# Turning the softmax's left-over columns and q as 64-row halves beside P's halves, and adding the softmax's constant on ScalarE

## The chip, the cores and the metric

The kernel runs on one core of one Trainium2 chip. The metric is the device time of one execution in microseconds, the median of three. The core has five engines that run side by side, each through its own list of instructions in order: TensorE (PE in the rows, its weight loads PEld), VectorE (DVE), ScalarE (ACT), GpSimd (POOL) and SyncE (SP, which here issues every DMA). They wait for one another through semaphores only.

## The reference, cut to what matters

Attention with a computed bias, then a feed-forward layer with a cosine gate, all in f32:

```
scores = scale * q @ k.T                       # batch 4, heads 8, sequence 576, head width 64
scores = scores + bias(head, row, column)      # a small two-layer net of log distances
scores = scores - max(scores, axis=-1)
attn   = exp(scores)
attn   = attn / (sum(attn, axis=-1) + 1e-09)
x      = (attn @ v), heads side by side        # 2304 x 512
h      = x @ w_in                              # 512 x 2048
out    = (h * cos(h)) @ w_out                  # 2304 x 512
```

## The kernel before, in words

The program has three stages: the bias tables (to about 66 us of the profiled span), attention (66 to 322 us), and the feed-forward layer (to the end). The change lies in attention alone.

Attention runs over 16 **units** `u`, each a pair of heads of one batch, and within a unit over 5 **slots** `j`. A slot takes one block of rows: `tiles = [0, 1, 4, 2, 3]`, so slots 0, 1, 3 and 4 take 128 rows of both heads, and slot 2 (tile 4) takes the last 64 rows of both heads together. `slot(i)` writes one step of a software pipeline over three jobs: `now` (job i), `last` (job i-1) and `prev` (job i-3). Each engine's list is written by hand in this order, and nothing reorders it.

TensorE's share of a slot, in order: the scores of `now` (`qk`, L394, tile `s`); the turning of `prev`'s probabilities P (`ptrans`, L456, tile `pm`); for the four tiles of 128 rows the **left-over**, columns 512 to 575 of both heads as one 128x128 block (`ptrans_left`, L469, tile `pt`); a turn of the next unit's inputs (`turn`, L188) in slots 0 to 2: k in slot 0 (four 128x128 blocks), x in slot 1 (the last 64 rows of k and q, one block), q in slot 2 (four blocks, into a spare tile of the score pool); and a part of the product with v of the unit before (`pv`, L518). P is turned by `flip` as 64-row halves: half r uses rows 64r to 64r+63 of the array and writes its own PSUM bank, `m0` or `m1`, so two halves run beside each other. Left-over, k, x and q go through the whole 128x128 array.

`ps_s`, the score pool, has two buffers: `s` of head 0 and of head 1. In slot 2 one holds that slot's scores and the other, `spare`, the turned q. So slot 3's scores of head 1 wait until ScalarE has read `spare`.

ScalarE's share of a slot: the exponentials of `last` (`softmax_exp`, L427), each followed by a read of its accumulated sum into `dn`; the copy of `m0` (`keep_main` 0, L476); then what was turned (`keep_turned`, L195, L198, L203); then a finished product (`keep_x`). VectorE's share: scores plus bias with their extreme value (L407); `dn` plus 1e-9 (L439) and its reciprocal `rc` (L442); the copy of `m1` and of the left-over (L479); steps that widen the feed-forward weights (L101 to L107). GpSimd scales P by `rc` (`norm`, L449) and splits the turned q and k in two parts (`split`, L174, L178). The split of q in slot 0 has to be done before slot 1 overwrites the tile of turned q (L198).

SyncE issues the loads in the order of the slots by `LOAD_PLAN`: q for the unit after next in slot 0, k for the third unit in slot 2 (two DMAs of the main part, two of the last 64 rows of k and q), v in slot 4 (four DMAs). In every fourth unit each slot also loads the next heads' bias (`load_bias`, three DMAs, two for tile 4). In slot 2 of odd units a weight part is loaded (`load_w`), which waits for VectorE's last widening step.

Of the kernel before, what the change touches and what calls it, by code (L numbers as in the profile page):

```python
# [9 lines left out]
F32 = mybir.dt.float32  # L10
# [3 lines left out]
AF = mybir.ActivationFunctionType  # L14
# [14 lines left out]
def kernel(  # L29
# [11 lines left out]
    nc = tc.nc  # L41
# [71 lines left out]
    with tc.manual_schedule():  # L113
# [11 lines left out]
        bp = opened(front, "bp", 11, "right")  # L125

        warm = const.tile([1, 1], F32, name="warm")
        nc.vector.memset(warm, 0.0)
# [11 lines left out]

        def load(u, x):
# [12 lines left out]
            m = 5 if x == "k" else 4  # L154
            t = (lk if x == "k" else ld).tile([128, m, 2, D], F32, tag=x, name=f"n{x}")
            for h in range(2):
                nc.sync.dma_start(out=t[:, 0:4, h], in_=pair_[h, 0:512].rearrange("(p r) d -> p r d", r=4))
            if x == "k":
# [4 lines left out]
            nat[u, x] = t  # L163

# [20 lines left out]
        def turn(u, x, ps):  # L185
# [3 lines left out]
            return ps  # L189

        def keep_turned(x, ps):
            if x == "x":
# [8 lines left out]
                return  # L201
            o = turned[x][:, 64:576] if x == "k" else turned[x][:, 0:512]
            nc.scalar.activation(  # L203
                out=o.rearrange("p (x c) -> p x c", c=4),
# [180 lines left out]
        def qk(u, j):  # L385
# [32 lines left out]
            if t == 4:  # L418
                return ps_s.tile([128, 2, 512], F32, tag="s", name="spare")[:, 0]

        P, dn, rc = {}, {}, {}

        def softmax_exp(u, j, h):
            neg, m = cur.pop((u, j, h))
            if h == 0:
# [7 lines left out]
                accum_out=dn[u, j][:, h : h + 1],  # L433
            )

        def recip(u, j, step):
            n = 2 if tiles[j] < 4 else 1
            if step == 0:
                nc.vector.tensor_scalar(dn[u, j][:, 0:n], dn[u, j][:, 0:n], 1e-9, None, ALU.add)  # L439
            else:  # L440
                rc[u, j] = sv.tile([128, 2], F32, tag="rc", name="rc")
                nc.vector.reciprocal(rc[u, j][:, 0:n], dn[u, j][:, 0:n])  # L442

# [10 lines left out]
        def flip(out, i, r):  # L454
            p = slice(64 * r, 64 * r + 64)
            nc.tensor.transpose(out, i[p], ident[p, p], tile_position=(64 * r, 0))  # L456

        def ptrans(u, j):
            ps = [ps_m.tile([128, 512], F32, tag=f"m{r}", name="pm") for r in range(2)]
            cuts = [(256 * h + 64 * c, 640 * h + 128 * c) for h in heads_of((u, j)) for c in range(4)]  # L460
            if tiles[j] == 4:
                cuts.append((256, 512))
            for o, i in cuts:
                for r in range(2):
                    flip(ps[r][:, o : o + 64], P[u, j][:, i : i + 128], r)
            return ps

        def ptrans_left(u, j, ps):
            nc.tensor.transpose(ps, P[u, j][:, 512:640], ident)  # L469

# [71 lines left out]
        PV_EARLY = [[(-1, 0, (0, 1))], [(-1, 0, (2, 3))], [(-1, 0, (4,))], [(-1, 1, (0, 1, 2))], [(-1, 1, (3, 4))]]  # L542
        LOAD_PLAN = [[(2, "q")], [], [(3, "k")], [], [(1, "v")]]
        W_PLAN = [("abs", -1), (0, 0), (0.5, 2), (1, 5), (2, 7), ("load", 7), (3, 8), (4, 11)]
        get = lambda i: jobs[i] if 0 <= i < len(jobs) else None

        def slot(i):
# [4 lines left out]
            if last:  # L552
                for h in heads_of(last):
                    softmax_exp(*last, h)
            if prev:
                if prev[1] in (0, 2):
                    alloc_half(prev[0], prev[1] // 2)
                pm = ptrans(*prev)
# [4 lines left out]
            if left:  # L563
                pl = t[:, 0:128]
                ptrans_left(*prev, pl)
            if tx:
                pt = turn(u + tu, tx, {"x": t and t[:, 128:256], "k": t, "q": spare}[tx])
            for du, hf, chunks in PV_EARLY[j]:
                if 0 <= u + du < NU:
                    pv(u + du, hf, chunks)  # L570
            if prev:
                keep_main(*prev, 0, pm[0])
            if tx:
                keep_turned(tx, pt)
# [3 lines left out]
            if last:  # L578
                recip(*last, 0)
                recip(*last, 1)  # L580
            if prev:
# [12 lines left out]
            if now:  # L594
                if i == 1:
                    load(0, "v")
                    load(2, "k")
                for du, x in LOAD_PLAN[j]:
                    if u + du < NU:
                        load(u + du, x)  # L600
                hp, b = units[u]
# [242 lines left out]
```

## Time and profile before

| | us |
|---|---|
| median of 3 runs | 727.86 |
| lowest and highest | 727.65, 728.61 |
| the profiled execution's own time | 730.44 |
| its span, first to last instruction | 728.6 |
| TensorE busy in the span | 712.5 |
| VectorE, ScalarE, GpSimd busy | 606.6, 443.9, 405.4 |

A group of the profile is named by line, engine, operation, `out<-in`, shape and count. A timeline row merges equal instructions that follow each other: its duration runs from the first start to the last end, and a bracket gives the engine's idle time before it and who ended it. Matmuls overlap, so what one costs is read from one start to the next, not from its duration.

### The profile page before, as it was taken

Reading aid. Unit: us, or ns where it says so; the run is one execution under the profiler, and the core shown is the slowest. Engines: PE = TensorE matmul, PEld = TensorE weight load, DVE = VectorE, ACT = ScalarE, POOL = GpSimd, SP = SyncE. Lnnn points to the kernel's source line nnn. Section 1 sums busy time; section 2 is a strip of 40 time slices with the busy share of each in tenths; the row PEclk is TensorE's granted clock in tenths of the full one; section 3 lists DMA queues with packets and bytes.
Section 4 is the critical chain, followed back from the end, with each engine's and each line's share of the span. In section 5 each row is a group of like instructions: output and inputs, shape, how many; then the busy total and the mean of one; then the engine's idle time right before and its main releaser. Section 6 shows DMA issues by size and latency. Waiting matters only on the chain.

```text
span 728.6 us, 15710 instructions
## 1 busy us (share of the span) xinstructions
PE 712.5 (98%) x5786; PEld 571.8 (78%) x5786; DVE 606.6 (83%) x1307; ACT 443.9 (61%) x947; POOL 405.4 (56%) x486
## 2 busy tenths in 40 slices
PE   6997999999999999999999999999999999999997
PEld 3575667766667667669989989988989989989986
DVE  8997788989889888856788789898999999966665
ACT  6897688787778878754565555445454454443342
POOL 0204678888877788874456373564554463663300
PEclk9999899999999999999999999999999999999999
DMA  6787328335432820201011010101011010011113
GB/s 202 239 303 210 91 66 229 78 82 141 135 94 64 232 47 18 76 1 30 30 50 38 32 57 29 59 30 58 30 35 53 29 59 30 0 43 45 45 43 88
DMA packets 84398, 58.65 MB, mean 80 GB/s; under 512 B 62304, under 2 KB 70624, under 8 KB 84320
## 3 DMA queue, kind: packets, MB, share of 16 engines
q1 hardware_dynamic: 84320, 57.63, 27.2%
q8 instruction: 46, 0.75, 0.4%
q14 instruction: 32, 0.26, 0.1%
HBM read 42.00 MB, written 15.61 MB: 79 GB/s over the span
## 4 chain that ended last, share of the span: by engine, by line
PE 95%; DVE 2%; POOL 1%; issue 1%; DMA 0%; ACT 0%; SPq 0%; DVEq 0%
PE ph L644 28%; PE po L699 28%; PE pv L518 13%; PE s L394 11%; PE pa L309 6%; PE pm L456 5%; PE pt L469 2%; PE pt L188 2%; DVE ht L293 1%; PE spare L188 1%; DMA lt<-in_ltab_dram 0%; POOL P L449 0%; DVE P L407 0%; DVE acc L722 0%; POOL kN L178 0%
## 5 line engine op out<-in xcount | busy, mean ns | idle before, releaser
L449 POOL TENSOR_SCALAR P<-P,rc 128x576 f32<-128x576 f32 x144 | 115.0, 812 | 75.7 <-ACT P L427 31.1
L407 DVE CUSTOM_DVE_ANT_0 P<-s,bt 128x576 f32<-128x576 f32 x144 | 103.8, 754 | 29.1 <-PE s L394 19.7
L648 ACT ACTIVATE a<-ph,quarter 128x384 int32<-128x384 f32 x96 | 55.8, 581 | 102.3 <-PE ph L644 101.0
L503 POOL TENSOR_TENSOR xs<-xT,xs 128x384 fp32r<-128x384 f32 x96 | 107.7, 1122 | 8.0
L427 ACT ACTIVATE P<-P,m 128x576 f32<-128x576 f32 x144 | 110.6, 771 | 2.1 <-DVE m L407 1.7
L644 PE MATMUL ph<-xs,wpre 128*128 128x384 f32 x576 | 109.4, 338 | 0.0
L654 DVE SCALAR_TENSOR_TENSOR r<-a,ph 128x384 f32<-128x384 int32 x96 | 52.8, 550 | 67.4 <-ACT a L648 67.2
L644 PE MATMUL ph<-xs,w 128*128 128x384 f32 x576 | 108.3, 337 | 0.0
L644 PEld LDWEIGHTS ph<-xs,wpre 128*128 128x128 f32 x576 | 101.8, 188 | 5.7 <-DVE a L663 0.9
L644 PEld LDWEIGHTS ph<-xs,w 128*128 128x128 f32 x576 | 101.5, 188 | 4.7 <-DVE a L663 0.6
L659 ACT ACTIVATE r<-r,hpi 128x384 f32<-128x384 f32 x96 | 59.3, 617 | 73.5 <-DVE r L655 73.3
L394 PEld LDWEIGHTS s<-kN,qT 64*128 64x128 f32 (+1 forms) x864 | 70.5, 188 | 40.8 <-issue 8.8
L394 PE MATMUL s<-kN,qT 64*128 64x288 f32 (+1 forms) x864 | 93.4, 315 | 4.0 <-DVE m L407 1.8
L502 POOL TENSOR_SCALAR xs<-xT 128x384 fp32r<-128x384 f32 x96 | 62.9, 656 | 39.9 <-PE ph L644 39.9
L518 PE MATMUL pv<-PT,vN 128*64 128x320 f32 (+1 forms) x512 | 76.9, 422 | 0.1
L673 DVE TENSOR_TENSOR gl<-a,gh 128x384 fp32r<-128x384 f32 x96 | 74.3, 774 | 2.2 <-ACT gh L667 2.2
L699 PE MATMUL po<-wpre,gh 128*128 128x512 f32 x288 | 75.3, 397 | 0.0
L699 PE MATMUL po<-w,gh 128*128 128x512 f32 x288 | 75.2, 395 | 0.0
L111 POOL TENSOR_TENSOR w<-wb,w 128x512 fp32r<-128x512 f32 x16 | 20.8, 1298 | 89.2 <-ACT w L109 89.2
L655 DVE SCALAR_TENSOR_TENSOR r<-a,r 128x384 f32<-128x384 int32 x96 | 60.6, 632 | 3.3
L667 ACT ACTIVATE gh<-a 128x384 fp32r<-128x384 f32 x96 | 49.8, 518 | 21.6 <-DVE a L663 21.6
L476 ACT ACTIVATE PT<-pm 128x512 f32<-128x512 f32 (+1 forms) x80 | 44.1, 551 | 30.8 <-PE pm L456 29.5
(83 smaller groups left out, 1220.1 us busy)
## 6 DMA issues: line engine op xcount, KB each, us to landing
sc<-rt SPq DMA_DIRECT2D x36, 295.5 KB, 3.3
raw<-in_moe_w_in_dram SPq DMA_DIRECT2D x16, 512.0 KB, 3.7
raw<-in_moe_w_out_dram SPq DMA_DIRECT2D x16, 512.0 KB, 3.6
bt<-sc SPq DMA_DIRECT2D x16, 288.0 KB, 4.0
nk<-in_k_dram SPq DMA_DIRECT2D x32, 128.0 KB, 3.1
nq<-in_q_dram SPq DMA_DIRECT2D x32, 128.0 KB, 2.9
bt<-sc SPq DMA_DIRECT2D x16, 256.0 KB, 4.0
vN<-in_v_dram SPq DMA_DIRECT2D x32, 128.0 KB, 2.6
```

The lines of the kernel that those rows point to most:

```text
L394: nc.tensor.matmul(s[h][:, hf, 0:HALF], qTs[u % 2][r, a, 128 * t : 128 * t + 128] if t < 4 else qTs[u % 2][:, a, 512:640], kN[u][r, b, o : ...
L407: nc.vector.tensor_tensor_reduce(neg.rearrange("p (a x) -> p a x", a=2), s[h][:, :, 0:HALF], bias[hp, t, h].rearrange("p (a x) -> p a x", ...
L427: nc.scalar.activation(out=P[u, j][:, 576 * h : 576 * h + 576], in_=neg, func=AF.Exp, bias=m[:, 0:1], scale=-1.0, accum_out=dn[u, j][:, h ...
L449: nc.gpsimd.tensor_scalar(p, p, r, 1.0, ALU.mult, ALU.mult)
L502: nc.gpsimd.tensor_scalar(h, src, 1.0, 1.0, ALU.mult, ALU.mult)
L503: nc.gpsimd.tensor_tensor(l, src, f(h), ALU.subtract)
L518: nc.tensor.matmul(ps[64 * h : 64 * h + 64, 0 : WQ[hf]], a, m, start=(c == 0), stop=(c == 4), tile_position=(r.start, 64 * h), skip_group_ ...
L644: nc.tensor.matmul(ps, a, x, start=(i == 0), stop=(i == 3 * KD - 1))
L655: nc.vector.scalar_tensor_tensor(r, n, -TWO_PI_LO, r, ALU.mult, ALU.add)
L659: nc.scalar.activation(out=r, in_=r, func=AF.Sin, scale=SIN_SCALE, bias=hpi)
L673: nc.vector.tensor_tensor(gl, a, f(G[key][0]), ALU.subtract)
L699: nc.tensor.matmul(O[n][i], a[:, 128 * i : 128 * i + 128], w, start=(i0 == 0 and p == 0), stop=(i0 == GF - 1 and p == 2),)
```

## The change

Left-over, x and q are turned by `flip` as halves too, in one list with P's halves (`halves`). For each half of the array a list is made; row 0's has the left-over (and x) behind its first P half, row 1's has them at its end; q's halves stand behind P's, with the two rows' results in the two banks of `spare`. The two lists are then interleaved pair by pair. The two halves of left-over and of x write the same PSUM bank, so an empty instruction on SyncE waits for row 0's last one and row 1's first one waits for it (`follow`). In the built program the empty instruction is one EVENT_SEMAPHORE, which waits for TensorE's semaphore and raises one that TensorE waits for. k is still turned whole; so are x and q where unit 0 turns them, since its slots 1 and 2 have no `prev`.

ScalarE adds 1e-9 to `dn` itself, behind the last exponential of a slot; VectorE keeps the reciprocal alone. The turned q is copied ahead of `m0`. k's load for the third unit is spread over slots 1 (main part) and 2 (last 64 rows).

```diff
+        eps = const.tile([128, 1], F32, name="eps")
+        nc.vector.memset(eps, 1e-9)
...
+        def side_by_side(u, x, ps):
+            n = nat[u, "k" if x == "x" else x].rearrange("p r h d -> p r (h d)")
+            if x == "x":
+                return {"one": [(ps, n[:, 4])]}
+            return {"two": [([ps[:, r, 64 * c : 64 * c + 64] for r in range(2)], n[:, c]) for c in range(4)]}
...
+            if h == heads_of((u, j))[-1]:
+                n = h + 1
+                nc.scalar.activation(out=dn[u, j][:, 0:n], in_=dn[u, j][:, 0:n], func=AF.Identity, bias=eps)
...
-            if step == 0:
-                nc.vector.tensor_scalar(dn[u, j][:, 0:n], dn[u, j][:, 0:n], 1e-9, None, ALU.add)
...
+        def follow(first, then):
+            tc.add_manual_dep(
+                then.ins,
+                first.ins.name,
+                mybir.DependencyInfo(mybir.DependencyClass.Sync, mybir.DependencyReason.DATA),
+                reason="row tiles share a bank",
+            )
+            return then
...
+        def halves(u, j, left, x):
             ps = [ps_m.tile([128, 512], F32, tag=f"m{r}", name="pm") for r in range(2)]
...
-            for o, i in cuts:
-                for r in range(2):
-                    flip(ps[r][:, o : o + 64], P[u, j][:, i : i + 128], r)
+            rows = []
+            for r in range(2):
+                at = slice(64 * r, 64 * r + 64)
+                main = [(ps[r][:, o : o + 64], P[u, j][:, i : i + 128]) for o, i in cuts]
+                one = [(left[:, at], P[u, j][:, 512:640])] if left is not None else []
+                one += [(o[:, at], i) for o, i in x.get("one", [])]
+                two = [(o[r], i) for o, i in x.get("two", [])]
+                rows.append(main[:1] + one + main[1:] + two if r == 0 else main + two + one)
+            made = [[flip(*pair_[r], r) for r in range(2)] for pair_ in zip(*rows)]
+            if one:
+                follow(follow(made[len(one)][0], nc.sync.nop()), made[-len(one)][1])
             return ps
-
-        def ptrans_left(u, j, ps):
-            nc.tensor.transpose(ps, P[u, j][:, 512:640], ident)
...
-        LOAD_PLAN = [[(2, "q")], [], [(3, "k")], [], [(1, "v")]]
+        LOAD_PLAN = [[(2, "q", None)], [(3, "k", 0)], [(3, "k", 1)], [], [(1, "v", None)]]
...
+            if tx == "q":
+                keep_turned(tx, pt)
             if prev:
                 keep_main(*prev, 0, pm[0])
-            if tx:
+            if tx and tx != "q":
                 keep_turned(tx, pt)
```

TensorE in slot 2 of a unit, before. `pm` are P's halves, `pt` the left-over, `spare` the turned q, `pv` the product with v:

```order
L456 MATMUL pm<-ident,P 128x64 [waits Activation_49]
L456 MATMUL pm<-ident,P 128x64 [waits DVE_49]
L456 MATMUL pm<-ident,P 128x64 x14
L469 MATMUL pt<-ident,P 128x128 [waits DVE_49]
L188 MATMUL spare<-ident,nq 128x128 [waits DMAHW3_49,DMAHW2_49]
L188 MATMUL spare<-ident,nq 128x128 x3
L518 MATMUL pv<-PX_3692,vN_110 64x256 [waits DMAHW5_49]
```

The same place after the change:

```order
L474 MATMUL pm<-ident,P 128x64 [waits Activation_49]
L474 MATMUL pm<-ident,P 128x64 [waits DVE_49]
L474 MATMUL pt<-ident,P 128x64 [waits DVE_49]
L474 MATMUL pm<-ident,P 128x64 x14
L474 MATMUL spare<-ident,nq 128x64 [waits DMAHW5_49,DMAHW4_49]
L474 MATMUL spare<-ident,nq 128x64 x7
L474 MATMUL pt<-ident,P 128x64 [waits SP_sequencer_49]
L550 MATMUL pv<-PX_4114,vN_113 64x256 [waits DMAHW2_49]
```

The 128x64 shapes are halves: one left-over half and eight halves of q have come into the row of P's halves, and the second left-over half waits for SyncE.

ScalarE in slots 1 and 2, before. `P,dn` are the exponentials, `PT` the copy of `m0`, `kt` and `qt` what was turned:

```order
L427 ACTIVATE P,dn<-P,m 128x576 x2
L476 ACTIVATE PT_3512<-pm 128x8x64
L195 ACTIVATE kt<-pt 128x64 x2
L198 ACTIVATE qt<-pt 64x64 x2
L427 ACTIVATE P,dn<-P,m 128x576 x2
L476 ACTIVATE PT_3512<-pm 128x8x64
L203 ACTIVATE qt<-spare 128x512
L476 ACTIVATE xT<-pv 128x256
```

After:

```order
L455 ACTIVATE dn<-dn,eps 128x2
L508 ACTIVATE PT_3611<-pm 128x8x64
L205 ACTIVATE kt<-pt 128x64 x2
L208 ACTIVATE qt<-pt 64x64 x2
L445 ACTIVATE P,dn<-P,m 128x576 x2
L455 ACTIVATE dn<-dn,eps 128x2
L214 ACTIVATE qt<-spare 128x512
L508 ACTIVATE PT_3611<-pm 128x8x64
L508 ACTIVATE xT<-pv 128x256
```

The small instruction on `dn` stands behind each slot's exponentials, and the copy of the turned q stands ahead of the copy of `m0`.

SyncE in slots 0 to 2 of a unit that loads bias (`bt`), before:

```order
L218 DMA bt<-sc_71 128x512
L218 DMA bt<-sc_72 128x576
L218 DMA bt<-sc_72 128x64
L218 DMA bt<-sc_72 128x512
L157 DMA nk<-in_k_dram 128x4x64 x2
L160 DMA nk<-in_k_dram 64x2x64
L160 DMA nk<-in_q_dram 64x2x64
L231 DMA bt<-sc_75 64x576 x2
```

After:

```order
L236 DMA bt<-sc_71 128x512
L162 DMA nk<-in_k_dram 128x4x64 x2
L236 DMA bt<-sc_72 128x576
L236 DMA bt<-sc_72 128x64
L236 DMA bt<-sc_72 128x512
L165 DMA nk<-in_k_dram 64x2x64
L165 DMA nk<-in_q_dram 64x2x64
L249 DMA bt<-sc_75 64x576 x2
```

The main part of k has moved between the bias of slot 0 and that of slot 1. The empty instructions, one for each left-over, stand in this list too but are not printed: they are written while TensorE's turns are, so each stands ahead of its own slot's loads and behind all loads of earlier slots.

## Rows read from the trace of the kernel before

**Rows 1.** Windows in attention: length, busy us of PE, PEld, DVE, ACT, POOL, clock, DMA

```profile
178.00:194.00 16.00, 15.97 (x184) 11.04 (x182) 13.60 (x39) 13.06 (x35) 12.54 (x16) 1.00 0.77 214
194.00:210.00 16.00, 15.98 (x182) 10.96 (x182) 14.48 (x43) 12.38 (x34) 13.29 (x19) 1.00 0.25 57
```

**Rows 2.** Timeline of TensorE, two units: start us, duration us, line, tiles, merged count

```profile
173.04 0.66 PE L456 MATMUL pm<-ident,P 64*128 64x64 f32 x16
...
204.75 0.66 PE L456 MATMUL pm<-ident,P 64*128 64x64 f32 x16
205.33 0.33 PE L469 MATMUL pt<-ident,P 128*128 128x128 f32 x1
205.50 0.27 PE L188 MATMUL pt<-ident,nk 128*128 128x128 f32 x1
205.70 1.08 PE L518 MATMUL pv<-PT,vN 128*64 128x256 f32 x8
...
207.71 0.76 PE L456 MATMUL pm<-ident,P 64*128 64x64 f32 x16
208.39 0.33 PE L469 MATMUL pt<-ident,P 128*128 128x128 f32 x1
208.56 0.60 PE L188 MATMUL spare<-ident,nq 128*128 128x128 f32 x4
209.09 0.65 PE L518 MATMUL pv<-PX,vN 64*64 64x256 f32 x4
209.67 1.50 PE L394 MATMUL s<-kN,qT 64*128 64x288 f32 x12
210.88 0.78 PE L456 MATMUL pm<-ident,P 64*128 64x64 f32 x16
211.59 0.33 PE L469 MATMUL pt<-ident,P 128*128 128x128 f32 x1
211.85 1.84 PE L518 MATMUL pv<-PT,vN 128*64 128x320 f32 x12
```

**Rows 3.** Source line of the row-tiled turns: duration ns min/median/max, first and last start

```profile
L456 PE MATMUL pm<-ident,P x1184: 213/223/312, 66.6 to 319.5; 64*128 64x64 f32 x198
```

**Rows 4.** Timeline of ScalarE around the turned q, in two units

```profile
191.06 0.45 ACT L198 ACTIVATE qt<-pt 64x64 f32<-64x64 f32 x2 [0.31 <-POOL qT L178]
...
206.84 0.45 ACT L198 ACTIVATE qt<-pt 64x64 f32<-64x64 f32 x2 [0.57 <-POOL qT L178]
...
208.75 0.19 ACT L427 ACTIVATION_READ_ACCUMULATOR P<-P,m 128x1 f32 x1
208.96 0.60 ACT L476 ACTIVATE PT<-pm 128x512 f32<-128x512 f32 x1
209.46 0.59 ACT L203 ACTIVATE qt<-spare 128x512 f32<-128x512 f32 x1
```

**Rows 5.** Group of ScalarE's smallest copies by line: busy us, mean ns

```profile
L195 ACT ACTIVATE kt<-pt 128x64 f32<-128x64 f32 x32 | 5.2, 220 | 0.2 <-PE pt L188 0.2
```

**Rows 6.** VectorE's added constant by source line: duration ns min/median/max

```profile
L439 DVE TENSOR_SCALAR dn<-dn x80: 141/165/1087, 63.8 to 312.3; 128x2 f32<-128x2 f32 x64, 128x1 f32<-128x1 f32 x16
```

**Rows 7.** Timeline of VectorE at the same place

```profile
208.97 0.53 DVE L439 TENSOR_SCALAR dn<-dn 128x2 f32<-128x2 f32 x1 [0.28 <-ACT P L427]
209.54 0.17 DVE L442 RECIPROCAL rc<-dn 128x2 f32<-128x2 f32 x1
```

**Rows 8.** Timeline of GpSimd behind that reciprocal

```profile
209.90 0.75 POOL L449 TENSOR_SCALAR P<-P,rc 128x576 f32<-128x576 f32 x1 [0.42 <-DVE rc L442]
```

**Rows 9.** Timeline of SyncE's DMA issues in a unit that loads bias, and two units later

```profile
172.90 2.99 SPq L218 DMA_DIRECT2D bt<-sc  x6
...
205.80 1.40 SPq L157 DMA_DIRECT2D nk<-in_k_dram  x2
...
211.24 0.37 SPq L81 DMA_DIRECT2D raw<-in_moe_w_in_dram  x1
```

**Rows 10.** Source line of v's loads on SyncE: the instructions that only wait, duration ns min/median/max

```profile
L148 SPq EVENT_SEMAPHORE  x28: 17/17/17, 85.5 to 295.1; - x28
```

More of the change, by code (lines that the diff above doesn't have):

```diff
@@ L139, with load @@
         nat = {}
-        def load(u, x):
+        def load(u, x, part=None):
             hp, b = units[u]
@@ L154, in load @@
             m = 5 if x == "k" else 4
[L155 to L158, printed above, removed]
+            if part in (None, 0):
+                nat[u, x] = (lk if x == "k" else ld).tile([128, m, 2, D], F32, tag=x, name=f"n{x}")
+            t = nat[u, x]
+            if part in (None, 0):
+                for h in range(2):
+                    nc.sync.dma_start(out=t[:, 0:4, h], in_=pair_[h, 0:512].rearrange("(p r) d -> p r d", r=4))
+            if x == "k" and part in (None, 1):
                 for i, o in ((k, 0), (q, 64)):
@@ L162, in load @@
                     )
-            nat[u, x] = t
         def split(u, x, step=None):
@@ L202, in keep_turned @@
             o = turned[x][:, 64:576] if x == "k" else turned[x][:, 0:512]
+            if len(ps.shape) == 3:
+                nc.scalar.activation(
+                    out=o.rearrange("p (r x c) -> p r x c", r=2, c=4),
+                    in_=ps[:, :, 0:256].rearrange("p r (c x) -> p r x c", c=4),
+                    func=AF.Copy,
+                    scale=-0.125 if x == "q" else 1.0,
+                )
+                return
             nc.scalar.activation(
@@ L418, in qk @@
             if t == 4:
-                return ps_s.tile([128, 2, 512], F32, tag="s", name="spare")[:, 0]
+                return ps_s.tile([128, 2, 512], F32, tag="s", name="spare")
         P, dn, rc = {}, {}, {}
@@ L434, in softmax_exp, with recip @@
             )
-        def recip(u, j, step):
+            if h == heads_of((u, j))[-1]:
+                n = h + 1
+                nc.scalar.activation(out=dn[u, j][:, 0:n], in_=dn[u, j][:, 0:n], func=AF.Identity, bias=eps)
+        def recip(u, j):
             n = 2 if tiles[j] < 4 else 1
-            if step == 0:
-                nc.vector.tensor_scalar(dn[u, j][:, 0:n], dn[u, j][:, 0:n], 1e-9, None, ALU.add)
-            else:
-                rc[u, j] = sv.tile([128, 2], F32, tag="rc", name="rc")
-                nc.vector.reciprocal(rc[u, j][:, 0:n], dn[u, j][:, 0:n])
+            rc[u, j] = sv.tile([128, 2], F32, tag="rc", name="rc")
+            nc.vector.reciprocal(rc[u, j][:, 0:n], dn[u, j][:, 0:n])
         def norm(u, j, h):
@@ L455, in flip @@
             p = slice(64 * r, 64 * r + 64)
-            nc.tensor.transpose(out, i[p], ident[p, p], tile_position=(64 * r, 0))
-        def ptrans(u, j):
+            return nc.tensor.transpose(out, i[p], ident[p, p], tile_position=(64 * r, 0))
+        def follow(first, then):
[4 more added lines that the diff above has]
+                reason="row tiles share a bank",
+            )
+            return then
+        def halves(u, j, left, x):
             ps = [ps_m.tile([128, 512], F32, tag=f"m{r}", name="pm") for r in range(2)]
@@ L554, in slot @@
                     softmax_exp(*last, h)
[L555 to L558, printed above, removed]
             left = prev and tiles[prev[1]] < 4
@@ L562, in slot @@
             t = bank() if left or tx in ("x", "k") else None
-            if left:
-                pl = t[:, 0:128]
-                ptrans_left(*prev, pl)
+            pl = t[:, 0:128] if left else None
             if tx:
-                pt = turn(u + tu, tx, {"x": t and t[:, 128:256], "k": t, "q": spare}[tx])
+                pt = {"x": t and t[:, 128:256], "k": t, "q": spare}[tx]
+                if tx == "q" and not prev:
+                    pt = spare[:, 0]
+            if prev:
+                if prev[1] in (0, 2):
+                    alloc_half(prev[0], prev[1] // 2)
+                pm = halves(*prev, pl, side_by_side(u + tu, tx, pt) if tx in ("x", "q") else {})
+            if tx and not (prev and tx in ("x", "q")):
+                turn(u + tu, tx, pt)
             for du, hf, chunks in PV_EARLY[j]:
@@ L578, in slot @@
             if last:
-                recip(*last, 0)
-                recip(*last, 1)
+                recip(*last)
             if prev:
@@ L597, in slot @@
                     load(2, "k")
-                for du, x in LOAD_PLAN[j]:
+                for du, x, part in LOAD_PLAN[j]:
                     if u + du < NU:
-                        load(u + du, x)
+                        load(u + du, x, part)
                 hp, b = units[u]
```

## The prediction

> **What bounds the kernel now.** I read the windows of the attention stage first, then TensorE's timeline through two units, then the timelines of ScalarE, VectorE, GpSimd and SyncE at the same places. The windows show TensorE busy for 15.97 and 15.98 us of 16 at the full clock, VectorE for 13.60 and 14.48, ScalarE for 13.06 and 12.38, GpSimd for 12.54 and 13.29 [rows 1]. Overlapping matmuls count as busy while they stand still, so this alone proves nothing; the timeline does. From one block's start to the next there is no hole in slot 1, and the same block comes again two units later, at 173.04 and 204.75: 31.71 us, 15.86 a unit [rows 2]. One place waits. In slot 3 the scores start at 209.67 and take until 210.88. Head 1's need the buffer in which q was turned, and ScalarE's copy of it ends at 209.46 + 0.59 = 210.05 [rows 2, 4]. So slots 3, 4 and 0 run at TensorE's own pace, and the start of slot 3 is set by a chain that ends on ScalarE.
>
> **TensorE: what a half saves.** In slot 1 the 16 half turns span 0.66 us, and one lasts 0.223 [rows 2, 3]: (0.66 - 0.223) / 7 = 0.062 from pair to pair. The last pair starts 0.44 after the first, and the next block 0.14 after that (205.33). The left-over then costs 0.17, x 0.20, and in slot 2 the left-over 0.17 and q 209.09 - 208.56 = 0.53 [rows 2]. In slot 3, where the product with v follows at once, the left-over costs 211.85 - 211.59 = 0.26; slot 4 has the same order. After the change each whole turn is one more pair, 0.062, and one change of shape to v's product stays. No row shows that change from half turns to v's product: the nearest give 0.14 (half turns to a whole one) and 0.26 (a whole one to v's product), and nothing excludes the plain 0.06. I take 0.14, since half turns stand ahead of it there too.
> The Trainium skill, "TensorEngine Tiling (Array Packing)", Key Properties, says that changing the tiling mode drains the array. By that rule the change at the end is paid whatever stood before it, and only one of two is saved, as I assume.
> Slots 3 and 4: 0.14 + 0.26 - 0.06 - 0.14 = 0.20 each (0.08 to 0.28). Slot 1: 0.14 + 0.17 + 0.20 - 0.12 - 0.14 = 0.25. Slot 2: 0.14 + 0.17 + 0.53 - 0.31 - 0.14 = 0.39. Slot 0 keeps its whole k. The 0.64 of slots 1 and 2 I cost at nothing: TensorE only reaches slot 3's scores earlier, and they wait for the copy of q. If that cover is gone, it is a gain (rival B).
>
> **ScalarE: the q copy earlier, 80 instructions more.** In slot 2 the last sum is read until 208.75 + 0.19 = 208.94; the copy of P's half follows at 208.96 and q's at 209.46 [rows 4]. Now q's comes first, behind the new instruction, which waits for the sum. Where VectorE waits for its own result it starts 0.04 later (208.97 + 0.53 to 209.54) [rows 7]; a small copy on ScalarE lasts 0.22 [rows 5]. The instruction so costs 0.04 (all but the wait overlapped) to 0.36 (with 0.10 for the sum's read, which otherwise overlaps half its 0.19); I take 0.26, the two rows added. Then q's copy starts 0.52 - 0.26 = 0.26 earlier. But two such instructions stand ahead of it since the unit's start. Their 0.52 falls into ScalarE's wait for GpSimd ahead of the copies of x, which is 0.57 in one unit and 0.31 in the other [rows 4]: 0 and 0.21 are left over. q's copy gains 0.26 and 0.05, 0.31 in two units.
> The Trainium skill speaks against the move: "ScalarE: Activation LUTs", Rules for kernel authors, gives additions to VectorE. By its figures for a bias read from a tile (280 ns and 0.833 per element, 93 overlapped) the instruction is 0.19 net, an estimate from that page, 0.23 with the wait; the sum would be some 0.8 us better.
>
> **VectorE and GpSimd.** VectorE loses 80 additions, 0.165 in the median, up to 1.09 where GpSimd is busy [rows 6]. That is off the path; the reciprocal at 209.54 comes at 208.94 + 0.26 + 0.04 = 209.24. GpSimd follows a reciprocal by 0.19 (209.71 to 209.90) [rows 7, 8], so it isn't later. The left-over's first half now needs its bank at the second pair, behind VectorE's copy of the slot before; where it waits is ahead of the q copy, so hidden too.
>
> **SyncE: 64 waits.** Row 0's left-over half starts one pair behind the first and row 1's eight pairs behind: 7 x 0.062 = 0.43 of room in slots 3 and 4, less 0.223 for the half itself [rows 3]: 0.21. SyncE follows TensorE by 0.03 (205.50 + 0.27 to 205.80) [rows 2, 9], its waiting instruction takes 0.02 [rows 10], and the way back is between 0.03 and GpSimd's 0.19: 0.08 to 0.24, a stall of 0 to 0.03; with both ways at 0.19 it is 0.19. I take 0.02 for the 32 of slots 3 and 4: 0.6 us. Slot 1 has a pair less room and is hidden.
> Dearer is what stands ahead of the empty instruction on SyncE. In odd units up to 11 a weight load ends slot 2. At 211.24 + 0.37 = 211.61 it is issued, and slot 3's second half is due at 210.88 + 0.43 = 211.31 [rows 2, 9]: 0.3 (0 to 0.5), in three units, 0.9 us; in the other three the bias decides. In units 3, 7 and 11 the bias loads take 2.99 / 6 = 0.50 each. Slot 0's end at 172.90 + 1.49 = 174.39 and slot 1's half is due at 173.04 + 0.43 = 173.47 [rows 2, 9]: 0.9 late, most of it hidden in the 0.64 ahead of q. In slot 2 two of k (0.70 each by 1.40 / 2), two of bias and a weight load make 2.8 against a slot of about 3.2, and slot 1 hands on up to 0.3: 0 to 0.8, I take 0.4, three times, 1.2 us. k's load in two parts costs nothing by itself: the same four DMAs.
>
> **The sum.** Two units gain 0.31 + 4 x 0.20 = 1.11. Units 2 to 14 are 6.5 pairs: 7.2. Unit 15 and the two slots behind it have six left-overs at 0.20: 1.2. Units 0 and 1, where loads still set the pace, I count at nothing. 8.4 less 0.6, 0.9 and 1.2 is 5.7. The feed-forward stage only moves earlier. The profiled execution took 730.44, the median is 2.58 lower: 730.44 - 5.7 = 724.7, and 722.1 beside the median of 727.86.
>
> **Rivals.** *A, this forecast*: 722.1, by the bounds (0.08 to 0.28 four times in two units, 0.04 to 0.36 for the instruction, stalls 0 to 8) 718.5 to 726.4.
> *B, the q copy is no longer the limit*: the new instruction overlaps, VectorE's shorter list brings the exponentials earlier, and TensorE keeps the 0.64 too: 1.04 x 13 + 1.2 - 2.7 = 12.0, 715.9. For it: VectorE is the busiest behind TensorE [rows 1]. Against: the chain to q's copy runs through GpSimd, which loses no work.
> *C, ScalarE becomes the bound*: at 0.36 each, q's copy gains 0.16 less 0.15 and 0.41 in the two kinds of unit, -0.24 a pair; 0.80 - 0.24 = 0.56, times 6.5 is 3.6, with 1.2 and the costs of 2.7 a gain of 2.1; with a third of a microsecond more in each bias and weight unit 1.0: 726.8, no change. For it: 13.06 of 16 before 1.3 more a unit and a shorter unit [rows 1].
> This is what the rule of the Trainium skill's page on ScalarE, cited above, would come to here.
> *D, slower: the way through SyncE.* With 0.19 each way the half comes 0.22 late (0.223 + 0.19 + 0.05 + 0.19 - 0.43), and TensorE, standing still, pays another 0.14 as at a change of shape: 0.36 x 32 = 11.5 instead of 0.6: 8.4 - 11.5 - 2.1 = -5.2, 733.1. It turns the sign from 6.3 / 32 = 0.20 a wait. Against: SyncE's 0.03 behind TensorE.
> That the halves don't run side by side has little for it: same shapes, same lists.
>
> **How the numbers follow.** A 0.52, B 0.22, C 0.15, D 0.11. The likeliest is A, 722.1. The range 715.0 to 729.0 leaves out D and a little of B. About 0.2% (1.5 us) is what a measurement of this kernel can tell from no change: faster 0.74 (A, B), same 0.15 (C), slower 0.11 (D).
>
> **What would show it.** In the profile after: no VectorE group on the added constant, a ScalarE group of 80 small ones at 0.2 to 0.3 each; q's copy 0 to 0.3 earlier in its unit; slots 3 and 4 with 0.2 less from half turns to v's product; the same block again after some 30.5 to 30.7 instead of 31.7. If TensorE's waits for SyncE come to more than 6 us in total, D holds; if ScalarE has no idle time ahead of the copies of x and q's copy comes later in its unit, C; if slot 3's scores no longer wait, B. The forecast is wrong if v's product costs more behind half turns than behind a whole one.

## The result and the profile after

| | before | after |
|---|---|---|
| median of five runs each, us | 728.03 | 734.53 |
| lowest and highest | 727.65, 728.61 | 731.36, 735.33 |
| profiled execution, its span | 730.44, 728.6 | 735.33, 733.5 |

The ratio is 1.0083 (95% interval 1.006 to 1.0106): slower by 0.8%, where 0.8% faster was forecast. The time lies outside the range.

The first view is the windows of two units that load no bias (length, then busy us of PE, PEld, DVE, ACT, POOL, clock and DMA), which answer to [rows 1].

```profile
205.53:220.82 15.29, 14.90 (x193) 10.46 (x192) 12.24 (x36) 13.69 (x38) 12.52 (x17) 1.00 0.38 94
220.82:236.43 15.61, 15.13 (x193) 10.62 (x191) 12.17 (x36) 13.73 (x38) 13.22 (x18) 1.00 0.26 59
```

Two units take 30.90 us; the first of them still holds a stall of 0.19 behind its weight load. The same two of the kernel before took 31.43, from first scores to first scores:

```profile
200.95 1.05 PE L394 MATMUL s<-kN,qT 64*128 64x288 f32 x12
...
232.38 0.79 PE L394 MATMUL s<-kN,qT 64*128 64x288 f32 x8
```

So the steady work did get shorter, and ScalarE is now busier than VectorE. The loss is elsewhere. The chain that ended last, on the profile's page, has two new names: SyncE, which had 0% of it before, has 3%, and ScalarE 7% where it also had 0%.

```profile
PE 82%; ACT 7%; SPq 3%; POOL 2%; DVE 2%; issue 2%; DMA 1%; DVEq 0%; POOLq 0%; ACTq 0%
```

The empty instruction's source line shows its duration and who waited for it (us, times):

```profile
L500 SPq EVENT_SEMAPHORE  x64: 17/17/17, 72.5 to 323.3; - x64
...
  PEld pt L474: 15.3, 14
  PE pt L474: 13.0, 8
```

Both lines tell of the same stalls, once at the weight load and once at the matmul, so TensorE stood still for some 15 us, nearly all of it in 14 of 64 places. Pair by pair, from row 0's half to row 1's, I find 16 stalls of more than 0.05 us, 15.9 us together. The other 48 cost nothing. This is what one of those looks like on TensorE (start, duration):

```profile
203.57 0.22 PE L474 MATMUL pt<-ident,P 64*128 64x64 f32 x1
203.63 0.53 PE L474 MATMUL pm<-ident,P 64*128 64x64 f32 x12
204.00 0.22 PE L474 MATMUL pt<-ident,P 64*128 64x64 f32 x1
204.00 0.22 PE L474 MATMUL pm<-ident,P 64*128 64x64 f32 x1
204.16 0.76 PE L550 MATMUL pv<-PT,vN 128*64 128x320 f32 x4
```

Row 0's half starts at 203.57 and row 1's at 204.00, seven pairs later, with nothing between them standing still. (7 x 0.062 = 0.43.) The product with v follows 0.16 behind, the change of shape that the prediction took at 0.14.

The largest stall is the first one. TensorE, then SyncE at the same time:

```profile
66.84 0.22 PE L474 MATMUL pt<-ident,P 64*128 64x64 f32 x1
66.90 0.66 PE L474 MATMUL pm<-ident,P 64*128 64x64 f32 x15
72.56 0.37 PE L474 MATMUL pt<-ident,P 64*128 64x64 f32 x1 [5.00 <-SPq L500]
```

```profile
65.97 1.15 SPq L154 DMA_DIRECT2D vN<-in_v_dram  x2
67.17 1.27 SPq L162 DMA_DIRECT2D nk<-in_k_dram  x2
68.48 0.63 SPq L165 DMA_DIRECT2D nk<-in_k_dram  x1
69.16 0.61 SPq L165 DMA_DIRECT2D nk<-in_q_dram  x1
69.87 1.24 SPq L162 DMA_DIRECT2D nk<-in_k_dram  x2
71.15 0.63 SPq L165 DMA_DIRECT2D nk<-in_k_dram  x1
71.83 0.62 SPq L165 DMA_DIRECT2D nk<-in_q_dram  x1
```

SyncE issues loads without a pause, at about 0.6 us each. Row 0's half was finished by 67.1, but the empty instruction stands behind the last load, which is issued by 72.45. Row 1's half starts 0.11 after that. In slot 3 of unit 7, a unit that loads bias, it is the same:

```profile
181.86 0.22 PE L474 MATMUL pt<-ident,P 64*128 64x64 f32 x1
181.92 0.66 PE L474 MATMUL pm<-ident,P 64*128 64x64 f32 x15
185.00 0.27 PE L474 MATMUL pt<-ident,P 64*128 64x64 f32 x1 [2.42 <-SPq L500]
```

```profile
180.80 2.17 SPq L165 DMA_DIRECT2D nk<-in_q_dram  x1
183.07 1.19 SPq L249 DMA_DIRECT2D bt<-sc  x2
184.37 0.53 SPq L86 DMA_DIRECT2D raw<-in_moe_w_out_dram  x1
```

One load of the last 64 rows holds SyncE for 2.17 us here, where such an issue takes 0.62 in the median. Two bias loads and the weight load follow, and all stand ahead of the empty instruction.

A stall of the first unit costs more than itself. The windows show what TensorE's clock does behind it (the number ahead of the last two):

```profile
66.00:70.00 4.00, 1.55 (x28) 1.42 (x28) 2.53 (x7) 3.34 (x9) 4.00 (x6) 1.00 0.78 174
70.00:74.00 4.00, 1.44 (x12) 1.45 (x14) 0.29 (x1) 0.07 (x1) 1.96 (x4) 0.63 0.49 109
74.00:78.00 4.00, 3.99 (x43) 3.53 (x42) 2.60 (x8) 2.40 (x6) 1.47 (x2) 0.50 0.32 72
78.00:82.00 4.00, 4.00 (x29) 2.42 (x28) 2.63 (x8) 2.89 (x8) 2.61 (x3) 0.59 0.32 71
```

TensorE is busy for 3.0 of 8 us, and the granted clock then goes to 0.50, the lower of the two levels (1.2 GHz). It is back at 1.00 only after 81. The profiled execution of the kernel before had a shorter dip at this place (0.79, 0.50 and 0.86 from 70 to 82), which began so:

```profile
70.00:74.00 4.00, 2.30 (x21) 1.93 (x22) 1.79 (x8) 1.91 (x5) 3.83 (x6) 0.79 0.47 103
```

The new ScalarE instruction by its source line (ns minimum, median, maximum), and around the turned q on ScalarE's timeline, in the unit that starts at 205.53. They answer to [rows 4 to 6].

```profile
L455 ACT ACTIVATE dn<-dn,eps x80: 294/295/298, 62.5 to 316.5; 128x2 f32<-128x2 f32 x64, 128x1 f32<-128x1 f32 x16
```

```profile
213.16 0.19 ACT L445 ACTIVATION_READ_ACCUMULATOR P<-P,m 128x1 f32 x1
213.38 0.29 ACT L455 ACTIVATE dn<-dn,eps 128x2 f32<-128x2 f32 x1
213.70 0.60 ACT L214 ACTIVATE qt<-spare 128x512 f32<-128x512 f32 x1
```

From the read of the sum to the copy of q it is 213.70 - 213.16 = 0.54. In the kernel before the copy that stood there followed the read by 208.96 - 208.75 = 0.21 [rows 4]. The instruction so takes 0.33 of ScalarE's time, near the upper end (0.36) of what the prediction allowed.

### The profile page after: what moved, and what is told of

The parts are those of the page before. It is cut to its first block, busy times and chain, and to the rows that moved or that the text cites. A ratio compares the mean times of both kernels' runs of the same rounds, so it can differ in the third digit from the quotient of the medians.

```text
span 733.5 us, 16055 instructions
## 1 busy us (share of the span) xinstructions
PE 702.1 (96%) x5920; PEld 568.1 (77%) x5920; DVE 583.7 (80%) x1228; ACT 463.1 (63%) x1027; POOL 405.9 (55%) x486
## 4 chain that ended last, share of the span: by engine, by line
PE 82%; ACT 7%; SPq 3%; POOL 2%; DVE 2%; issue 2%; DMA 1%; DVEq 0%; POOLq 0%; ACTq 0%
PE ph L679 28%; PE po L734 27%; PE pv L550 9%; PE s L412 7%; PE pa L327 6%; PE pm L474 3%; ACT P L445 3%; SPq L162 1%; POOL P L467 1%; PE pt L474 1%; DVE ht L311 1%; SPq L236 1%; ACT PT L508 1%; PE pt L192 1%; ACT qt L214 1%
## 5 line engine op out<-in xcount | busy, mean ns | idle before, releaser
L474 PE MATMUL pm<-ident,P 64*128 64x64 f32 x1184 | 60.9, 226 | 0.6 <-POOL P L467 0.6
```

The source lines that it names most:

```text
L474: return nc.tensor.transpose(out, i[p], ident[p, p], tile_position=(64 * r, 0))
```

## The experiments

Two explanations were held against each other. **S**: what SyncE has ahead of the empty instruction makes the loss, and the rest brings about what was forecast. The other, A in the first expectations: the gain itself is missing, because ScalarE's instruction or the early copy of q doesn't bring what was reckoned. H there is a third: half turns cost more than whole ones. Two numbers of each run's trace are told below its expectations: units 0 and 1 together, and units 2 to 14 together, both from the starts of the units' first scores on TensorE's timeline. The kernel before has 32.0 and 204.6, where the profiled execution had the dip of the clock. The changed kernel has 34.6 and 207.1. The feed-forward stage takes 401 to 402 us in every kernel. Left-overs waited for on TensorE itself, without SyncE, were not tried, so the price of that is open.

**1. Left-over and x whole where SyncE's list is long** (unit 0, the bias units, slot 1 behind them):

```
-                pm = halves(*prev, pl, side_by_side(u + tu, tx, pt) if tx in ("x", "q") else {})
+                late = (u == 0 or u % B == B - 1 or (u % B == 0 and j == 1)) and u < NU - 1
+                beside = tx == "q" or (tx == "x" and not late)
+                pm = halves(*prev, None if late else pl, side_by_side(u + tu, tx, pt) if beside else {})
+                if late and left:
+                    nc.tensor.transpose(pl, P[prev][:, 512:640], ident)
...
```

> The changed kernel, but the left-over (and x in slot 1) is turned whole, without SyncE's instruction, in unit 0, in units 3, 7 and 11, and in slot 1 of the units behind these: 14 of the places where TensorE stood for SyncE, 15.4 us of the 16.0 us that I add up from the trace of the changed kernel. Theory S (the loss is TensorE waiting behind DMA issues on SyncE): the waits fall under 1 us in total and the time to 717 to 721. Theory A (the 0.295 us instruction on ScalarE eats the gain and the waits only stand where TensorE would wait anyway): 729 to 734. Theory H (half turns cost more than whole ones beside v's product): 733 or more.

Measured: 724.36, ratio 0.9941 (0.9919 to 0.9964). Three stalls are left, 0.5 us together. Units 0 and 1 take 29.6 and units 2 to 14 201.1, 11.0 us less than in the changed kernel; the medians differ by 10.2. S holds for the sign: without the stalls the change is faster, and A (729 or more) and H (733 or more) fall. It isn't the 717 to 721 that S would give if the steady gain were the forecast one.

**2. The constant on ScalarE and nothing else**, in the kernel before:

```
...
+            if h == heads_of((u, j))[-1]:
+                n = h + 1
+                nc.scalar.activation(out=dn[u, j][:, 0:n], in_=dn[u, j][:, 0:n], func=AF.Identity, bias=eps)
...
-            if step == 0:
-                nc.vector.tensor_scalar(dn[u, j][:, 0:n], dn[u, j][:, 0:n], 1e-9, None, ALU.add)
...
```

> The kernel before with one part of the change: ScalarE adds the constant, VectorE keeps the reciprocal; everything is turned as before. Theory A: slower than before by 5 us or more (80 x 0.295 is 23.6 us of ScalarE, a third of it on the path to the copy of q). Theory S: within 4 us of before, either way.

Measured: 734.25, ratio 1.0082 (1.0062 to 1.0102). Alone it costs as much as the whole change: A's mark is met, and S's (within 4 us) is not. Units 2 to 14 take 210.9, 6.4 more than before, and two units 32.41. Slot 3's scores tell why:

```profile
226.57 0.40 PE L396 MATMUL s<-kN,qT 64*128 64x288 f32 x1
227.60 0.93 PE L396 MATMUL s<-kN,qT 64*128 64x288 f32 x10 [0.64 <-ACT qt L205]
```

Head 1's scores stand still for the turned q, which ScalarE copies last. Three new instructions of a unit at 0.33 each stand ahead of that copy, 1.0 us. Counted from the unit's first scores, the copy comes 0.84 later than before in even units and 0.14 later in odd ones, 0.98 in two units, which take 0.99 more.

**3. The changed kernel with the constant on VectorE** (the edit above, undone):

> The changed kernel with the constant added on VectorE as before. Theory A: 725 or less. Theory S: TensorE's waits for SyncE stay at 14 to 18 us and the time within 4 us of 734.5.

Measured: 734.95, ratio 1.009 (1.0063 to 1.0116). The time is the changed kernel's, and 15 stalls of 15.5 us stay, so S holds and A falls. Units 2 to 14 take 205.5, 1.6 less, but units 0 and 1 take 35.2, 0.6 more, and the end of attention takes 0.7 more. So the constant, which cost 6.4 us by itself in run 2, hardly shows in the time of the changed kernel. Whether it is the stalls that hide it is for run 6 to say.

**4. q alone as halves and copied early, the constant on ScalarE, left-over and x whole:**

```
-                pm = halves(*prev, pl, side_by_side(u + tu, tx, pt) if tx in ("x", "q") else {})
+                pm = halves(*prev, None, side_by_side(u + tu, tx, pt) if tx == "q" else {})
+                if left:
+                    nc.tensor.transpose(pl, P[prev][:, 512:640], ident)
...
```

> The changed kernel with left-over and x turned whole everywhere, so that q's halves, the order of ScalarE's copies and the constant remain and SyncE has no such instruction. Theory S: faster than before, 721 to 726, by the part of the gain that is q's and the copies'. Theory A: no faster than before, 728 or more. Theory H: slower than before by what q's halves cost.

Measured: 727.31, ratio 0.9988 (0.9977 to 1.0). It lies between what S gave (721 to 726) and what A gave (728 or more). Units 2 to 14 take 204.6, as before: what q gains, the constant takes (run 10 has the constant back).

**5. The stalls taken away by spreading the loads.** The changed kernel with 16 bias buffers for 11, the bias loads issued a few at a time in slot 3 of four units, the weight load moved to slot 3, and unit 0's first left-over whole:

```
-        bp = opened(front, "bp", 11, "right")
+        bp = opened(front, "bp", 16, "right")
...
-        W_PLAN = [..., ("load", 7), ...]
+        W_PLAN = [..., ("load", 8), ...]
...
-                pm = halves(*prev, pl, side_by_side(u + tu, tx, pt) if tx in ("x", "q") else {})
+                late = u == 0 and j == 3
+                pm = halves(*prev, None if late else pl, side_by_side(u + tu, tx, pt) if tx in ("x", "q") else {})
+                if late:
+                    nc.tensor.transpose(pl, P[prev][:, 512:640], ident)
...
-                if b == B - 1 and hp + 1 < HP:
-                    load_bias(hp + 1, tiles[j])
+                if j == 3 and hp + 1 < HP:
+                    if b == 0:
+                        waiting.extend(x for t_ in tiles for x in bias_parts(hp + 1, t_))
+                    for _ in range(((4, 3, 4, 3) if hp else (0, 5, 5, 4))[b]):
+                        waiting.pop(0)()
```

> The changed kernel, all halves kept, but SyncE freed ahead of its empty instructions: the bias loads of the next heads are spread over slot 3 of four units (16 bias buffers instead of 11), the weight load stands in slot 3 instead of 2, and unit 0's first left-over is turned whole. Theory S: TensorE's waits for SyncE fall from 16 us to under 1, and the time to 718 to 724 (the clean units of the changed kernel take 15.05 and 15.61 us, against 15.78 and 15.65 before). Theory A: no better than the kernel with the left-overs whole at the late places, 724.4 or more.

Measured: 725.14, ratio 0.9956 (0.9941 to 0.9971). That is faster than before by 0.4%, but over S's 718 to 724, and the 724.4 or more that A gave is met, so that the time alone doesn't decide. One stall is left, 2.6 us, in unit 0's next left-over. Units 2 to 14 take 199.9, and every pair from unit 2 on 30.70. The first scores of units 8 and 10:

```profile
182.77 1.07 PE L437 MATMUL s<-kN,qT 64*128 64x288 f32 x12
...
213.46 1.06 PE L437 MATMUL s<-kN,qT 64*128 64x288 f32 x12
```

So the steady gain of the change as it is made is 31.43 - 30.70 = 0.73 a pair, where 1.11 was forecast. In this kernel odd units take 15.07 and even ones 15.63. Before they took 15.78 and 15.65: the even units gain nothing. ScalarE shows why, in the unit that starts at 213.46:

```profile
219.75 0.45 ACT L208 ACTIVATE qt<-pt 64x64 f32<-64x64 f32 x2
220.22 0.78 ACT L470 ACTIVATE P<-P,m 128x576 f32<-128x576 f32 x1
...
221.89 0.30 ACT L480 ACTIVATE dn<-dn,eps 128x2 f32<-128x2 f32 x1
222.21 0.60 ACT L214 ACTIVATE qt<-spare 128x512 f32<-128x512 f32 x1
```

There is no bracket in its list from 213.93 on, so it works without a pause, and the copy of q comes 222.21 - 213.46 = 8.75 after the unit's first scores. In the kernel before the same unit had it at 225.12 - 216.73 = 8.39:

```profile
216.73 1.06 PE L394 MATMUL s<-kN,qT 64*128 64x288 f32 x12
225.12 0.59 ACT L203 ACTIVATE qt<-spare 128x512 f32<-128x512 f32 x1
```

In run 5 TensorE waits 0.42 for that copy.

**6. The same with the constant on VectorE:**

> The same with the constant on VectorE as before. The constant on ScalarE alone cost 6.4 us in the kernel before. If ScalarE limits the units here as well, this is 3 to 6 us faster than the one with the spread loads: 715 to 720. If q's copy ahead has already taken ScalarE off the path, the two are within 1.5 us.

Measured: 724.02, ratio 0.994 (0.9923 to 0.9958). Units 2 to 14 take 198.6, a pair 30.46: without the stalls the constant's place is worth 1.2 us there, and 1.1 in the median, so the second expectation (within 1.5 us) holds. With the stalls, from the changed kernel to run 3, the same units gave 1.6. So it isn't the stalls that hide the constant's price; the halves and q's earlier copy have lowered it. One stall of 3.6 us is left in unit 0.

**7. The wait alone**, in the kernel before: P's last half turn waits for an empty SyncE instruction that waits for the first one.

```
...
-            for o, i in cuts:
-                for r in range(2):
-                    flip(ps[r][:, o : o + 64], P[u, j][:, i : i + 128], r)
+            made = [[flip(ps[r][:, o : o + 64], P[u, j][:, i : i + 128], r) for r in range(2)] for o, i in cuts]
+            if tiles[j] < 4:
+                follow(follow(made[0][0], nc.sync.nop()), made[-1][1])
```

> The kernel before with the wait alone: in the four slots with a left-over, the last half turn of P in row 1 waits for an empty SyncE instruction that waits for the first half turn in row 0; everything is turned, copied and loaded as before. Theory S: TensorE waits for SyncE in unit 0, in the units that load bias and behind them, and at weight loads, 10 to 18 us in total, and the time rises by 6 to 15 us, to 734 to 743. Theory A: within 2 us of before.

Measured: 746.14, ratio 1.0242 (1.0222 to 1.0261), above the range that S gave. Units 0 and 1 take 34.2, units 2 to 14 215.9, 11.4 more than before. The source line of the empty instruction:

```profile
  PEld pm L456: 15.4, 15
  PE pm L456: 12.7, 10
```

The stalls are as many and as long as those of the changed kernel. So the wait by itself loses all that the changed kernel loses to it, and more, with no gain set against it.

**8. Run 5 with q copied behind P's half:**

```
-            if tx == "q":
-                keep_turned(tx, pt)
             if prev:
                 keep_main(*prev, 0, pm[0])
-            if tx and tx != "q":
+            if tx:
                 keep_turned(tx, pt)
```

> The kernel with the spread loads, with one thing undone: ScalarE copies the turned q behind P's half, as before the change. If q's copy sets the start of slot 3, as the prediction has it, each unit is longer by 0.3 to 0.5 us: 4 to 7 us slower than with the copy ahead. If not, within 1.5 us.

Measured: 731.91, ratio 1.0054 (1.0037 to 1.0071), 6.8 us over run 5; units 2 to 14 take 206.4, 6.6 more. Slot 3's head 1 now waits 0.86 to 0.90 us for that copy. The order of the two copies is worth what the prediction built on it: 0.5 us a unit.

**9. Run 6 with all of unit 0's left-overs whole**, which is also the best kernel found:

```
-                late = u == 0 and j == 3
+                late = u == 0 and left
```

> e7_spread_dve with the left-overs of unit 0 whole in all its slots (e7 had only the first one whole; the next one then waited 3.6 us, and unit 0 took 14.9 us against 11.85 before). Theory S, what SyncE's list costs is all that is left of the loss: unit 0 returns to 11.9 us, TensorE's waits for SyncE in the trace fall under 0.6 us, and the time goes from e7's 724.0 to 720-721.5. Rival T, the start is bound elsewhere (by loads or GpSimd's splits, and the clock that falls with TensorE's idling): what unit 0 gains comes back in unit 1 (17.0 us there becomes about 20), and the time stays at 723.5-724.5.

Measured: 722.95 (721.81 to 724.14), ratio 0.993 (0.991 to 0.995). In the trace unit 0 does what S gave: it takes 11.82, and units 0 and 1 together 28.9 for 31.9, with one wait for SyncE of 0.7 us left (S gave under 0.6). Unit 1 takes 17.05 and not the 20 of rival T, so T falls there. All four executions lie above S's 720 to 721.5, though. Two had a mean granted clock of 1.000 and took 721.8, two had 0.994 and took 724.1. That the clock makes the difference isn't shown: in run 10 an execution at 0.995 took 724.7 and two at 1.000 took 724.5 and 724.7. In the profiled one, with 1.000, the windows from 70 to 78 read:

```profile
70.00:74.00 4.00, 2.35 (x26) 1.79 (x26) 2.34 (x9) 2.25 (x6) 3.91 (x6) 1.00 0.46 104
74.00:78.00 4.00, 3.43 (x47) 2.46 (x47) 3.89 (x12) 2.58 (x8) 2.54 (x4) 1.00 0.52 118
```

TensorE is still idle for 1.65 us of the first window here, nearly as in the kernel before (1.70), where the clock fell. What decides between the two isn't settled.

**10. q alone, the constant on VectorE** (run 4 with the constant moved back):

> e5_q_only with the constant back on VectorE: q as halves and its copy ahead of P's half, left-overs and x whole, no wait for SyncE. If the ScalarE instruction costs the same wherever it stands (before to e3_const_only: 31.43 to 32.41 us a pair of units, 0.98), two units take 30.45 us here instead of e5's 31.42, and the time is 727.3 - 6.5 = 720-721.5. Rival: its cost depends on what else ScalarE carries (e6 to e7: 30.70 to 30.48, only 0.22 a pair); then a pair takes 31.2 us and the time is 725.3-726.3.

Measured: 724.69, ratio 0.9953 (0.9938 to 0.9968), between the two expectations; units 2 to 14 take 201.3. Units 10 and 12 start 30.89 us apart, 0.54 less than in run 4.

**11. Run 9 with q whole and copied behind P's half**, so left-overs and x alone as halves, the constant on VectorE:

```
-                pm = halves(*prev, None if late else pl, side_by_side(u + tu, tx, pt) if tx in ("x", "q") else {})
+                pm = halves(*prev, None if late else pl, side_by_side(u + tu, tx, pt) if tx == "x" and not late else {})
...
```

> e10 with q turned whole and copied behind P's half, as in the kernel before: left-overs and x as halves, with SyncE's wait, loads spread, constant on VectorE. If the early copy of q is worth what e9 showed (1.0 us a pair of units), a pair takes 31.4-31.5 us and the time is 6-7 us above e10: 727-728, no faster than before, so that the left-overs' halves bring nothing by themselves. Rival: the halves of the left-overs shorten each unit on TensorE's side by what the prediction's working had (0.2 a slot); then a pair takes 30.9 and the time is 723-724.5.

Measured: 724.72, ratio 0.9958 (0.9941 to 0.9974); units 2 to 14 take 200.6, a pair 30.82. The first expectation falls, and the rival's 723 to 724.5 is missed by 0.2: left-overs and x as halves shorten a pair by 0.6 even with q late.

**12. The changed kernel with unit 0's left-overs whole and nothing else:**

> The changed kernel with the left-overs of unit 0 whole and nothing else altered: the bias loads still stand ahead of the empty instruction, the constant is still ScalarE's. Theory S, the loss is two separate stretches of SyncE's list: unit 0 returns from 16.8 us to 11.9, units 3, 7 and 11 and the ones behind them keep their 0.9 to 2.1 us over the clean 15.6 and 15.1, TensorE's waits for SyncE fall from 15.3 to some 10 us, and the time from 734.5 to 729-730.5. Rival, the stall of unit 0 is no loss because loads set the pace there anyway: unit 1 gets back what unit 0 gains, and the time stays over 733.

Measured: 730.62, ratio 1.0026 (1.001 to 1.0043). That is just above S's 729 to 730.5. Units 0 and 1 take 29.3, 5.3 less (unit 0 12.85, where S gave 11.9); units 2 to 14 208.2. The view of waits (us in total, times, longest) keeps the bias units' stalls:

```profile
PEld pt L474 <- SPq L500: 9.1, 13, 2.0
```

The rival falls: the stall of unit 0 is a loss, of about 4 us in the median.

Units 10 and 11 of the kernel before and of six runs in which no stall touches them, put side by side. Runs 5, 9 and 11 have the loads spread as well:

| us for two units | constant on VectorE | on ScalarE | constant costs |
|---|---|---|---|
| nothing as halves | 31.42 (before) | 32.41 (run 2) | 0.99 |
| q as halves, copied early | 30.89 (run 10) | 31.43 (run 4) | 0.54 |
| left-overs and x as halves | 30.82 (run 11) | - | - |
| all of them | 30.43 (run 9) | 30.70 (run 5) | 0.27 |

The constant costs most where q's copy is late, and less the more is turned as halves, though never nothing.

## Why the prediction was wrong

**The SyncE term failed, in size and in place.** It had two parts. The way through SyncE was put at 0.02 for a wait, and that is right: 48 of 64 waits cost nothing, since SyncE's instruction is done 0.28 to 0.40 us after the start of row 0's half and the room is 0.43. What stands ahead of the empty instruction was put at 0.9 for the weight loads and 1.2 for the bias units. The weight loads measured 0.5 (0.17, 0.15, 0.19). The bias units and the slot behind them measured 10.2: the prediction added issue times of 0.5 to 0.7 each, let most of the lateness of slots 0 and 1 fall into TensorE's wait ahead of q, and carried at most 0.3 of SyncE's lateness from one slot to the next. In the trace it grows through the unit up to slot 3, and a load that waits for a buffer or takes 2.17 us passes on to the next slot. After what is hidden, this costs 7.2 us: units 2 to 14 take 207.1 here and 199.9 in run 5.

**Units 0 and 1 were counted at nothing because loads set the pace there. That is the step that failed outright: it has no price in the prediction.** Loads setting the pace means that SyncE has a list of DMAs to issue, and the wait stands behind it. The first left-over waited 5.2 us, units 0 and 1 took 34.6 us for 29.1 (run 2, whose clock did not fall), and the median lost some 4 us by it (run 12). The same remark that made the prediction leave the stage out should have been the reason to look there. The rows of SyncE's timeline in the first unit were in the trace of before, where SyncE issues loads from 62.09 to 77.17 nearly without a pause, and they weren't among those it used:

```profile
70.87 1.24 SPq L157 DMA_DIRECT2D nk<-in_k_dram  x2
```

**The steady gain was over-sized, on ScalarE.** The new instruction takes 0.33 and not 0.26, and three stand ahead of each copy of q. The wait in which two of them were to vanish, 0.57 and 0.31 in the two kinds of unit [rows 4], was sampled badly: the 0.31 is of unit 8, behind a bias unit. (The prediction's 31.71 for two units spans the same unit; other pairs take 31.43.) In the other even units of the kernel before ScalarE has next to no idle time there, 0.03 to 0.05, too little for a bracket:

```profile
222.50 0.45 ACT L198 ACTIVATE qt<-pt 64x64 f32<-64x64 f32 x2
```

In even units q's copy comes 0.36 later instead of 0.05 earlier. In odd ones it comes 0.34 earlier, where 0.26 was forecast: 209.46 - 200.95 = 8.51 before, 213.70 - 205.53 = 8.17 after. So a pair gained 0.73, not 1.11, and units 2 to 14 4.7 us, not 7.2. Case C's mechanism was at work in every second unit, at 0.33 instead of its 0.36.

With the constant on VectorE (run 9) slot 3's scores hardly wait for q any more, the mark of case B, but a pair gains 0.99 and not B's 2 x 1.04 = 2.08. In its units 10 and 11 slots 1 and 4 are about 0.25 and 0.20 shorter than before, as forecast. But slot 0 is 0.16 to 0.19 longer, and in unit 10 slot 3 is 0.30 longer, where TensorE now waits for VectorE's copy:

```profile
219.66 0.27 PE L497 MATMUL pm<-ident,P 64*128 64x64 f32 x1 [0.21 <-DVE PT L534]
```

The Trainium skill's rule that additions belong to VectorE ("ScalarE: Activation LUTs", Rules for kernel authors) would have been the better guide: in this kernel it is worth 0.27 us in two units, 0.99 with nothing else changed. By the page's figures, as the prediction used them, the instruction would have been 0.23, an estimate; it was 0.33.

**Unit 15 and the tail** were to gain 1.2. From unit 15's first scores to one and the same product of the feed-forward layer (its first `po<-wpre,gl`) it is 31.4 us instead of 32.1, a gain of 0.7. It comes with the constant on ScalarE (31.4 in run 2 too) and not with the halves (32.1 in run 9). Run 5, with both and the loads spread, has 30.7, and why isn't known.

**What was right.** A change of shape at the end of a turned block costs 0.15 to 0.16 (0.14 was taken), the halves follow each other at 0.062, and the order of q's copy decides 6.8 us (run 8). Case D, the only slower one, had the sign and nearly the size (733.1), but by another mechanism, so that the size agrees is luck. It charged each of 32 waits 0.36 for the way there and back. The mark that the prediction set for it, more than 6 us of waits for SyncE, is met, with 15 us in 14 places. So the mark told apart too little: the way costs nothing, and the queue ahead costs all.

**The sum, with what was measured** (the profile): units 2 to 14 gain 4.7 and the tail 0.7. SyncE's list costs 7.2 in the bias and weight units, and 2.6 in units 0 and 1, which is 5.5 against a start without the clock's dip. In the two profiled executions 207.1 - 204.6 = 2.5, 34.6 - 32.0 = 2.6 and -0.7 make 4.4 of the 4.9 by which they differ. The other 0.5 is 0.6 more in the feed-forward stage, which the change doesn't touch, less 0.1 ahead of the first scores. Measured against the forecast, SyncE in the bias and weight units cost 4.5 more than its 2.7, units 0 and 1 some 4 (run 12's median), the steady gain was 2.5 short and the tail 0.5: 11.5 of the 12.4 between 722.1 and the median.

## What to carry to other kernels

An empty instruction on the engine that issues the loads costs what that engine has yet to issue ahead of it: before using such an engine to pass a signal, follow its list through the units where loads come in bunches, the first ones above all. An instruction is priced by the time until the next one can start, on the engine that has least idle time in that kind of unit, and idle time is read in every kind of unit and not in one. What one part of a change costs depends on the other parts: in units 2 to 14 the constant cost 6.4 us by itself, 3.3 with q as halves and copied early, and 1.2 with everything as halves.

## What the runs showed that was not expected

- Adding a bias from a tile to 128x2 elements holds ScalarE for 0.295 us by its record, and 0.33 from the instruction ahead to the one behind. VectorE's addition took 0.165 in the median [rows 6].
- A short wait in the first unit was followed by a spell at the lower level of the clock in one trace and not in another: TensorE was busy for 2.30 of the 4 us from 70 in the kernel before, and the clock went to 0.50; it was busy for 2.35 in run 9, and the clock stayed at 1.00.
- One DMA issue on SyncE lasted 2.17 us where its like takes 0.62 in the median, in the middle of a unit that loads bias. What holds it is open.
